# An attention-plus-MLP kernel rewritten: transposed Q, K and O, scores ahead of PV, paced side work

## The chip, the cores and the metric

The kernel runs on one core of a Trainium2 chip. The metric is the device time of one execution in microseconds (us). The profile tells apart a matrix engine (PE, or TensorE; the kernels here put its results into eight PSUM banks), ScalarE (ACT, which computes the exponentials here), VectorE (DVE), GpSimd (POOL) and queues for data movement. In the traces an engine takes its own instructions in the order of its queue and waits for the others: in the changed kernel ScalarE's normalisation of the third tile of x, whose inputs were ready at 10.6 us, started at 16.62 us, behind a copy of the tile before it that had waited 3.41 us for the PE. The profile also records the clock that the PE was granted; every record is either full or half (mean 0.617 before).

"Faster", "slower" and "same" below compare fast runs of two kernels on the same chip, in the same rounds. A ratio is the mean time of one kernel's fast runs over that of the other's of the same rounds, so it is not quite the ratio of the medians that stand beside it.

## The reference, cut to what matters

```python
xn = layernorm(x)                            # x: 2048 x 512, bf16
q = xn @ wq   # 32 heads of 16               k = xn @ wk ; v = xn @ wv   # one head of 16
p = softmax(q k^T / 4) ; o = p v             # 32 heads x 2048 x 2048 exponentials
out = x + o @ wo + (gelu(xn @ w1 + b1) @ w2 + b2)      # w1: 512 x 1792
```

The exponentials dominate: 32 x 2048 x 2048 of them, all on ScalarE in tiles of 128 rows, 948.7 us of the 1216.8 us span of the kernel before.

## The kernel before

A "chunk" is 512 query rows, one head with one query each: four heads by the same 128 queries. Three chunks form a group; a group takes 16 steps, one for each 128 keys. A step has three score matmuls (K is stationary, 17 rows: 16 for the head and one that subtracts a bound of the maximum), one exponential over three PSUM banks, and three PV matmuls that add up in the single O bank (V with a column of ones, so that row 16 of the result is the softmax denominator). There are 43 groups, 688 steps. The scores use six banks, two sets of three. All the rest of the PE's work (Q projection, GELU layer, output; "side work") uses the last bank.

```python
def plan_scores(s):          # three matmuls, side by side in three row strips of the array
    ...
        KT_sb[32*j:32*j+17, kt*P:(kt+1)*P], QT_sb[32*j:32*j+17, g % QT_RING, :]
def plan_PV(s):              # three matmuls side by side in three column strips, and a filler
    ...
        pO[32*j:32*j+17, :], V1[:, kt, :], E_sb[:, s % 2, j*512:(j+1)*512]
    if PV_FILL:
        pO[96:113, :], V1[:, kt, :], E_sb[:, s % 2, 0:512]       # its result is not used
def plan_O_evac(g):          # the O bank is free after these two
    t1 = tensor_copy(oc_hi, pO)                  # waits for the last PV of the group
    t_dveO[g] = tensor_tensor(oc_lo, pO, oc_hi, SUBTRACT)
...
for s in range(NS):          # order of the PE's queue
    plan_exp(s)
    plan_PV(s)
    if kt == KT - 1: plan_O_evac(g)
    if s + 2 < NS: plan_scores(s + 2)
    run_misc_slot(s)         # side work: now and then a burst, often of four or more matmuls
```

## Time and profile before

| | before |
|---|---|
| time | 1213.67 us, median of 3 (1209.01 to 1217.55) |
| first exponential starts, last ends | 65.0, 1207.4 us |
| ScalarE idle before exponentials, in between | 171 us |
| mean granted PE clock | 0.617 of full |

The page of the kernel before: its span, busy times (share of the span, number of instructions), the granted clock in tenths of full speed in 40 slices of the span, and some of the costliest groups. A group's line has the source line, engine, operation, result and inputs, sizes, count | busy us, mean ns | idle us of the engine just before, and who ended most of that.

```profile
span 1216.8 us, 14581 instructions
...
PE 960.1 (79%) x6411; PEld 237.8 (20%) x6477; DVE 356.8 (29%) x774; ACT 983.7 (81%) x763; POOL 99.1 (8%) x52
...
PEclk9855767668555557595666557755655595555555
...
L574 ACT ACTIVATE E_sb<-pAll 128x1536 bf16<-128x1536 f32 (+1 forms) x688 | 948.7, 1442 | 184.4 <-PE pAll L560 180.8
L593 PE MATMUL pAll<-E_sb,V 128*17 128x512 bf16 x2048 | 385.4, 552 | 118.5 <-ACT E_sb L574 115.8
L560 PE MATMUL pAll<-QT_sb,KT_sb 17*128 17x512 bf16 x2048 | 384.8, 553 | 0.0
...
L614 DVE CAST oc_hi<-pAll 128x512 bf16<-128x512 f32 x43 | 29.6, 689 | 258.2 <-PE pAll L598 258.2
...
L616 DVE TENSOR_TENSOR oc_lo<-pAll,oc_hi 128x512 bf16<-128x512 f32 x43 | 29.7, 691 | 1.5
```

ScalarE is the busiest engine and its exponentials waited 184 us in total, 181 of it for the scores (L560). The clock row shows 5 for most of the run: half clock, with stretches of full. The sum of idle time before the k-th exponential of a group, over all groups, is mine, from the trace: 72.7 us fall on the third exponential, 98 us on all others.

Timeline of the kernel before (start, length, engine, line, operation, count, idle before and who ended it); a burst of side-by-side matmuls is one line.

```profile
1165.12 0.60 PE L593 MATMUL pAll<-E_sb,V 128*17 128x512 bf16 x3 [0.21 <-ACT E_sb L574]
...
1165.78 0.69 DVE L614 CAST oc_hi<-pAll 128x512 bf16<-128x512 f32 x1 [18.75 <-PE pAll L598]
1166.50 0.69 DVE L616 TENSOR_TENSOR oc_lo<-pAll,oc_hi 128x512 bf16<-128x512 f32 x1
...
1167.71 0.60 PE L593 MATMUL pAll<-E_sb,V 128*17 128x512 bf16 x3
...
1168.25 0.61 PE L560 MATMUL pAll<-QT_sb,KT_sb 17*128 17x512 bf16 x3
...
1168.91 1.45 ACT L574 ACTIVATE E_sb<-pAll 128x1536 bf16<-128x1536 f32 x1 [1.14 <-PE pAll L560]
```

The last PV of the group (L593) starts at 1165.12. The two copies hold the O bank until 1167.2, the next PV starts at 1167.71, and the scores that ScalarE needs stand behind that PV: ScalarE is idle for 1.14 us.

### The profile page before, as it was taken

To read this page: it belongs to the slowest core of one execution; us is meant where nothing else is said; L and a number is where in the kernel's file an instruction comes from. 1 tells how busy PE (TensorE), PEld (TensorE's weight loads), DVE (VectorE), ACT (ScalarE), POOL (GpSimd) and SP (SyncE) were. 2 spreads that over 40 slices of the span, in tenths; PEclk is the share of its full clock that TensorE was granted. 3 is DMA by queue.
4 is the path that set the end of the run, shared out by engine and by line. 5 is a ranking of instruction groups with operands and counts; after the bars stand their busy time and mean duration, and the time that the engine had idled before them with its cause. 6 is when DMAs were issued, how large, how long until landed. Compare 5 with 4: busy or idle time off the path is not lost.

```text
span 1216.8 us, 14581 instructions
## 1 busy us (share of the span) xinstructions
PE 960.1 (79%) x6411; PEld 237.8 (20%) x6477; DVE 356.8 (29%) x774; ACT 983.7 (81%) x763; POOL 99.1 (8%) x52
## 2 busy tenths in 40 slices
PE   0578777779888887798887878888788888878887
PEld 0312122212112112121122112211122121111111
DVE  4634544431122344210244431112444121111101
ACT  0367879898987688899988789996887889988895
POOL 2268830000000000000000000000000000000000
PEclk9855767668555557595666557755655595555555
DMA  6000000000000000000000000000000000000000
GB/s 225 1 1 1 1 1 1 1 1 1 1 5 14 1 1 1 1 1 1 9 5 1 5 1 1 1 1 10 1 5 1 5 1 1 5 1 5 5 1 4
DMA packets 7326, 9.87 MB, mean 8 GB/s; under 512 B 448, under 2 KB 6880, under 8 KB 7264
## 3 DMA queue, kind: packets, MB, share of 16 engines
q1 hardware_dynamic: 6720, 6.55, 1.7%
q0 software_dynamic: 544, 2.40, 0.5%
q8 instruction: 50, 0.82, 0.3%
q14 instruction: 12, 0.10, 0.0%
HBM read 6.85 MB, written 2.10 MB: 7 GB/s over the span
## 4 chain that ended last, share of the span: by engine, by line
PE 43%; ACT 40%; DVE 11%; issue 3%; DMA 1%; POOL 1%; SPq 0%
ACT E_sb L574 39%; PE pAll L593 12%; PE pAll L560 11%; PE pAll L741 6%; PE pAll L794 5%; DVE oc_lo L616 2%; DVE oc_hi L614 2%; PE pAll L700 2%; PE pAll L508 2%; PE pAll L402 1%; DMA x_sb<-in_A_x_dram 1%; PE pAll L634 1%; POOL m_f L431 1%; ACT ub L767 1%; DVE xpy L802 1%
## 5 line engine op out<-in xcount | busy, mean ns | idle before, releaser
L574 ACT ACTIVATE E_sb<-pAll 128x1536 bf16<-128x1536 f32 (+1 forms) x688 | 948.7, 1442 | 184.4 <-PE pAll L560 180.8
L593 PE MATMUL pAll<-E_sb,V 128*17 128x512 bf16 x2048 | 385.4, 552 | 118.5 <-ACT E_sb L574 115.8
L560 PE MATMUL pAll<-QT_sb,KT_sb 17*128 17x512 bf16 x2048 | 384.8, 553 | 0.0
L598 PE MATMUL pAll<-E_sb,V 128*17 128x512 bf16 x688 | 379.2, 551 | 0.0
L593 PEld LDWEIGHTS pAll<-E_sb,V 128*17 128x17 bf16 x2048 | 69.4, 93 | 431.7 <-ACT E_sb L574 335.2
L560 PEld LDWEIGHTS pAll<-QT_sb,KT_sb 17*128 17x128 bf16 x2048 | 71.1, 97 | 272.1 <-issue 272.1
L614 DVE CAST oc_hi<-pAll 128x512 bf16<-128x512 f32 x43 | 29.6, 689 | 258.2 <-PE pAll L598 258.2
L748 DVE TENSOR_SCALAR hb<-pAll,b1T 128x512 bf16<-128x512 f32 x56 | 42.0, 751 | 184.0 <-PE pAll L741 184.0
L741 PE MATMUL pAll<-xnT,w_sb 128*128 128x512 bf16 x197 | 84.2, 567 | 10.1 <-issue 7.6
L431 POOL TENSOR_TENSOR m_f<-ssqR,half_sb 128x32 f32<-128x32 f32 x16 | 86.8, 5426 | 44.3 <-DVE ssqR L428 44.3
L794 PE MATMUL pAll<-w_sb,ub 128*128 128x512 bf16 x208 | 64.6, 415 | 6.6 <-DVE xpy L802 4.4
L598 PEld LDWEIGHTS pAll<-E_sb,V 128*17 128x17 bf16 x688 | 61.6, 90 | 0.0
L634 PE MATMUL pAll<-ident_b,oc_hi 81*128 81x51 bf16 (+1 forms) x172 | 19.6, 215 | 50.2 <-DVE oc_lo L616 48.3
L774 DVE SCALAR_TENSOR_TENSOR ub<-ub,hb 128x512 bf16<-128x512 bf16 x56 | 38.4, 686 | 44.8 <-ACT ub L767 44.8
L802 DVE TENSOR_TENSOR xpy<-pAll,x_sb 128x512 f32<-128x512 f32 x16 | 11.1, 692 | 110.2 <-PE pAll L798 110.2
L516 DVE CAST QT_sb<-pAll 81x512 bf16<-81x512 f32 (+1 forms) x43 | 29.5, 685 | 39.5 <-PE pAll L598 28.2
L508 PE MATMUL pAll<-ident_b,qx 128*17 128x128 bf16 x512 | 26.9, 298 | 17.0 <-POOL qx L434 9.6
L767 ACT ACTIVATE ub<-ub 128x512 bf16<-128x512 bf16 x56 | 35.2, 628 | 0.0
L285 ACT ACTIVATE xnT<-pAll 128x512 bf16<-128x512 f32 x16 | 9.6, 597 | 30.0 <-PE pAll L280 29.6
L707 DVE TENSOR_TENSOR outbuf<-pAll,xpy 128x512 bf16<-128x512 f32 x16 | 11.1, 692 | 75.4 <-PE pAll L700 75.4
L741 PEld LDWEIGHTS pAll<-xnT,w_sb 128*128 128x128 bf16 x224 | 22.4, 121 | 48.6 <-issue 42.6
L616 DVE TENSOR_TENSOR oc_lo<-pAll,oc_hi 128x512 bf16<-128x512 f32 x43 | 29.7, 691 | 1.5
(83 smaller groups left out, 372.6 us busy)
## 6 DMA issues: line engine op xcount, KB each, us to landing
x_sb<-in_A_x_dram SPq DMA_DIRECT2D x2, 1024.0 KB, 10.7
out_dram<-outbuf SPq DMA_DIRECT2D x16, 128.0 KB, 1.7
w_sb<-in_B_w_dram SPq DMA_DIRECT2D x1, 1792.0 KB, 19.8
w_sb<-in_B_w_dram POOLq DMA_DIRECT2D x1, 1792.0 KB, 12.4
wq_sb<-in_A_wq_dram POOLq DMA_DIRECT2D x1, 512.0 KB, 7.8
wo_sb<-in_A_wo_dram SPq DMA_DIRECT2D x1, 512.0 KB, 19.1
wkv_sb<-in_A_wk_dram POOLq DMA_DIRECT2D x1, 16.0 KB, 6.7
wkv_sb<-in_A_wv_dram POOLq DMA_DIRECT2D x1, 16.0 KB, 6.6
```

The lines of the kernel that those rows point to most:

```text
L431: tpw = add("pool", (lambda ti: lambda e: e.tensor_tensor(m_f[:, ti, :], ssqR[:, ti, :], half_sb[:, :], ALU.pow))(ti), waits=[("dve", tR), ...
L508: tk = add("pe", (lambda j, qb, tc, h: lambda e: e.matmul(pM[32 * j:32 * j + 17, qb * P:(qb + 1) * P], qx[:, tc, h, :], ident_b[:, :]))(j, ...
L560: tk = add("pe", (lambda j, X, kt, g: lambda e: e.matmul(pS[:, (3 * X + j) * 512:(3 * X + j + 1) * 512], KT_sb[32 * j:32 * j + 17, kt * P: ...
L574: t_actE[s] = add("act", (lambda X, n, s: lambda e: e.activation(E_sb[:, s % 2, 0:n * 512], pS[:, 3 * X * 512: 3 * X * 512 + n * 512], ACT ...
L593: tk = add("pe", (lambda j, kt, s: lambda e: e.matmul(pO[32 * j:32 * j + 17, :], V1[:, kt, :], E_sb[:, s % 2, j * 512:(j + 1) * 512], star ...
L598: tk = add("pe", (lambda kt, s: lambda e: e.matmul(pO[96:113, :], V1[:, kt, :], E_sb[:, s % 2, 0:512], start=(kt == 0), stop=(kt == KT - 1 ...
L614: t1 = add("dve", (lambda g: lambda e: e.tensor_copy(oc_hi[:, g % 2, :], pO[:, :]))(g), waits=waits, mark=True)
L616: t_dveO[g] = add("dve", (lambda g: lambda e: e.tensor_tensor(oc_lo[:, g % 2, :], pO[:, :], oc_hi[:, g % 2, :], ALU.subtract))(g), waits=[ ...
L741: tk = add("pe", (lambda d, ft, c0, c1, w, pb: lambda e: e.matmul(pb[:, 0:w], w1_sb[:, d, ft * P:(ft + 1) * P], xnT[:, d, c0:c1], start=(d ...
L748: th = add("dve", (lambda ft, w, pb: lambda e: e.tensor_scalar(hb[:, ft, 0:w], pb[:, 0:w], b1T[:, ft:ft + 1], None, ALU.add))(ft, w, pb), ...
L767: t_actT[(sc, ft)] = add("act", (lambda ft, w: lambda e: e.activation(ub[:, ft, 0:w], ub[:, ft, 0:w], ACT.Tanh, scale=GELU_K))(ft, w), wai ...
L794: tk = add("pe", (lambda ft, loc: lambda e: e.matmul(pM[:, :], ub[:, ft, loc * P:(loc + 1) * P], w2_sb[:, ft, :], start=(ft == 0), stop=Fa ...
```

## The change

Its intent: keep everything transposed so that no PE transposes are needed, put the scores ahead of PV in the PE's queue so that ScalarE's next exponential is never behind PV, pace the side work to two matmuls per step, and normalise in batches of four tiles. A new bookkeeper (`Prog`) derives the semaphore waits from what each operation reads (`r=`) and writes (`w=`). Groups are three heads by the same 512 tokens, so there are 4 x 11 groups (the eleventh has two heads) and 704 steps. The diff is 1449 lines; this is its core.

```diff
-            plan_exp(s)
-            plan_PV(s)
-            if kt == KT - 1: plan_O_evac(g)
-            if s + 2 < NS: plan_scores(s + 2)
-            run_misc_slot(s)
+            exp(s)
+            if s + 2 < NS:
+                scores(s + 2)
+            pv(s)                       # E has four buffers; no filler matmul
+            if kt == NT - 1:
+                o_evac(tb, g)
+            ...                         # tanh in threes, gates
+            while mi_live and n < PER_STEP and s >= gap_until:     # PER_STEP = 2
+                k = next(mi)            # one side matmul
...
+        def scores(s):
+                mm(bank(3 * x + j), KT[q0:q0 + 17, kt * P:(kt + 1) * P], QT[q0:q0 + 17, tb % 2, h // 4, :], ...)
+        def pv(s):
+                mm(pO[32 * j:32 * j + 32, :], V1[:, kt, :], E[:, s % NEB, j * TBW:(j + 1) * TBW], ...)
+        def o_evac(tb, g):
+            dve(stream_shuffle(den[0:n, i, :], pO[0:n, :], [16] * 32), w=[B(6), ("den", i)])
+            dve(reciprocal(den[0:n, i, :], den[0:n, i, :]), ...)
+            dve(tensor_tensor(oT[0:n, tb % 2, g, :], pO[0:n, :], den[0:n, i, :], MULT), w=[B(6), ...])
...
+        ln_batch(0); consts_dve(); ln_batch(1); k_block(0); ...; ln_batch(2); k_block(1); ln_batch(3); ...
```

B(6) is the O bank. All three operations of `o_evac` touch it or stand between two that do, so the next PV waits for all three. The padding rows 17 to 31 of KT and QT are zero, because the projection weights are padded with zero columns.

## The prediction

> **What bounds it now.** Page: span 1216.8 us, ScalarE (ACT) busy 984 (81%), PE 960 (79%). Groups: 672 exponentials of 128x1536, back to back every 1.35 us (timeline), 16 of 128x1024 at about 0.93, 56 tanh at about 0.53: a floor of about 952 us. The first exponential starts at 65 us, the last ends at 1207 (timeline, chain of waits). So ACT waits about 190 us in the loop, 181 of it on the scores. Two causes. (a) PE order PV, scores, then a side burst of four matmuls: when the clock is half (mean 0.617) PV takes 0.53, scores 0.54, a burst 1.8 us, and ACT loses 1.44 us, as at 83 to 112 us. (b) At each of 43 group ends the two O copies (0.69 + 0.69) hold the O bank, then eight transposes precede the next PV: about 1 us lost.
>
> **What the change does.**
> - Exponential work is unchanged: 640 of 1536, 64 of 1024, tanh in threes (20): about 950 us.
> - Prologue: the first exponential at about 45 us instead of 65. The GpSimd power (2 x 5.4 us) and K/Q transposes go; but the GpSimd half of the normalisation stands behind two large memsets (about 10 us, estimated from its small memsets), and ACT's in-order queue waits for it. -20.
> - Scores ahead of PV, at most two side matmuls per step: PE per step is 0.32 + 0.32 + 0.53 = 1.17 us at full clock, under 1.35: no loss. At half clock 0.53 + 0.54 + 0.96 = 2.0, over it. On average there are 1.07 side matmuls per step, so half-clock stretches remain PE bound. I give this 30 to 70 us, against 120 to 140 for (a) now.
> - Group end: shuffle 0.69, reciprocal, multiply 0.69 hold the O bank. The small reciprocals took 207 ns for 8 elements, 233 for 12, 253 for 16: about 155 + 6.4 ns per element, so 512 should take about 3.4 us. [...] The next PV can start about 5.6 us after the last exponential's end. ACT has three exponentials ready (4.1 us), then waits for PV, side work and scores: 2.4 to 3.7 us lost, and the 4 us of PE idleness also drop the clock. 43 x about 3 = 130 us against about 43 now.
> - Tail: about 44 Y/output matmuls are left after the last step: about 18 us against 9.
>
> Sum: 45 + 950 + 130 + 40 + 15 = 1180. I take 1178 us, 80% range 1105 to 1245. Chances: faster by over 2% 0.55, within 0.31, slower 0.14.
>
> **What would show it.** Right: the reciprocal group at 3 to 4 us each, 44 of them; ACT's idle time before exponentials in pieces of 2 to 4 us about every 25 us; PV waiting for the O multiply; first exponential at 40 to 50 us; between group ends, exponentials every 1.35 us in full-clock stretches. Wrong: a reciprocal near 0.7 us (then the group ends cost almost nothing, and about 1060 is right); ACT idle spread over all steps (then PE bounds it).
>
> **What would make it wrong.** A clock mostly at half: the Y stretches, two side matmuls in every step, then run at 2.0 us per step, and 1230 or more follows. VectorE work queued ahead of the O evacuation lengthens the hold.

## The result

The changed kernel took 1345.45 us (median of 4 runs, 1339.45 to 1357.83) against 1211.93 (4 runs): ratio 1.110, 95% interval 1.103 to 1.116. It is 11% slower. The result is correct.

The page of the changed kernel. L222 is a helper through which all of its matmuls go, so they are told apart by their tiles.

```profile
span 1340.7 us, 11668 instructions
...
PE 1061.3 (79%) x4964; PEld 208.6 (16%) x5029; DVE 447.0 (33%) x642; ACT 998.7 (74%) x758; POOL 17.4 (1%) x26
...
PEclk9655555555557865555556865555558655755557
...
L387 ACT ACTIVATE E<-pAll 128x1536 bf16<-128x1536 f32 (+1 forms) x704 | 953.8, 1425 | 285.9 <-PE pAll L222 277.1
L222 PE MATMUL pAll<-E,V 128*32 128x512 bf16 x2048 | 409.5, 575 | 178.5 <-DVE oT L401 178.5
L222 PE MATMUL pAll<-QT,KT 17*128 17x512 bf16 x2048 | 404.1, 567 | 39.3 <-ACT E L387 31.8
L400 DVE RECIPROCAL den<-den 96x512 f32<-96x512 f32 (+1 forms) x44 | 147.3, 3349 | 1.5
...
L399 DVE STREAM_SHUFFLE den<-pAll 96x512 f32<-96x512 f32 (+1 forms) x44 | 31.7, 720 | 0.0
L401 DVE TENSOR_TENSOR oT<-pAll,den 96x512 bf16<-96x512 f32 (+1 forms) x44 | 30.2, 686 | 1.5
```

Three things to read here. ScalarE's idle time before exponentials went up, from 184 to 286 us, nearly all of it waiting for the PE. The clock row is almost all fives. The reciprocal is one instruction of 3349 ns for each group, as predicted, and PV waited 178.5 us for the multiply (L401) that ends the hold of the O bank.

The timeline of the changed kernel around one group end, with the half-clock steps before it and the change to full clock after it:

```profile
709.14 0.61 PE L222 MATMUL pAll<-QT,KT 17*128 17x512 bf16 x3
...
709.68 0.61 PE L222 MATMUL pAll<-E,V 128*32 128x512 bf16 x3
709.80 1.45 ACT L387 ACTIVATE E<-pAll 128x1536 bf16<-128x1536 f32 x1 [0.60 <-PE pAll L222]
...
710.23 1.03 PE L222 MATMUL pAll<-wop,oT 96*128 96x512 bf16 x2
...
711.20 0.61 PE L222 MATMUL pAll<-QT,KT 17*128 17x512 bf16 x3
...
714.51 0.72 DVE L399 STREAM_SHUFFLE den<-pAll 96x512 f32<-96x512 f32 x1
715.26 3.35 DVE L400 RECIPROCAL den<-den 96x512 f32<-96x512 f32 x1
...
718.65 0.69 DVE L401 TENSOR_TENSOR oT<-pAll,den 96x512 bf16<-96x512 f32 x1
...
719.39 0.61 PE L222 MATMUL pAll<-E,V 128*32 128x512 bf16 x3 [3.48 <-DVE oT L401]
...
720.47 0.61 PE L222 MATMUL pAll<-QT,KT 17*128 17x512 bf16 x3
...
721.13 2.79 ACT L387 ACTIVATE E<-pAll 128x1536 bf16<-128x1536 f32 x2 [3.72 <-PE pAll L222]
...
727.72 0.39 PE L222 MATMUL pAll<-QT,KT 17*128 17x512 bf16 x3
...
728.16 16.23 ACT L387 ACTIVATE E<-pAll 128x1536 bf16<-128x1536 f32 x12 [0.38 <-PE pAll L222]
...
728.91 0.39 PE L222 MATMUL pAll<-QT,KT 17*128 17x512 bf16 x3
```

Between 709 and 714 a step takes 2.06 us (709.14 to 711.20): scores 0.54, PV 0.55, two side matmuls 0.97, and ScalarE is idle 0.60 us in each step. From 693 to 715 the PE is never free, and yet the clock stays at half: its records give half clock from 645.8 to 727.8. Then the same four bursts take 1.19 us (727.72 to 728.91) and ScalarE runs twelve exponentials without a stop. In between is the group end: shuffle at 714.51, reciprocal until 718.61, multiply until 719.34, next PV at 719.39, scores after it at 720.47, and ScalarE idle for 3.72 us.

All traces, read the same way. "At the group end" is the idle time before the fourth exponential of a group if scores go ahead of PV, before the third if PV goes first; "elsewhere" is that before all other exponentials. "No wait" is the time from the first exponential to the end of the last, less idle. All in us, one profiled execution each.

| kernel | span | clock | first exponential | idle at the group end | idle elsewhere | no wait | after the last |
|---|---|---|---|---|---|---|---|
| before | 1216.8 | 0.617 | 65.0 | 72.7 | 98 | 972 | 9.5 |
| changed | 1340.7 | 0.578 | 62.4 | 169.8 | 112 | 978 | 18.9 |

The difference of the spans, 124 us, is 97 at the group ends, 14 elsewhere, 6 of no wait, 9 after the last exponential, and -3 at the start.

### The profile page after: what moved, and what is told of

Read it like the earlier page. It is cut to its first block, busy times and chain, and to the rows that moved or that the text cites. A ratio compares the mean times of both kernels' runs of the same rounds, so it can differ in the third digit from the quotient of the medians.

```text
span 1340.7 us, 11668 instructions
## 1 busy us (share of the span) xinstructions
PE 1061.3 (79%) x4964; PEld 208.6 (16%) x5029; DVE 447.0 (33%) x642; ACT 998.7 (74%) x758; POOL 17.4 (1%) x26
## 4 chain that ended last, share of the span: by engine, by line
PE 61%; ACT 19%; DVE 17%; issue 2%; POOL 1%; DMA 0%; DVEq 0%
PE pAll L222 61%; ACT E L387 16%; DVE den L400 11%; DVE den L399 2%; DVE oT L401 2%; ACT ub L441 1%; PE pAll L298 0%; ACT xn L289 0%; ACT xnT L301 0%; POOL wop L257 0%; DVE stats L277 0%; DMA wk_s<-in_A_wk_dram 0%; POOL wqp L256 0%; ACT KT L311 0%; DVE outb L568 0%
## 5 line engine op out<-in xcount | busy, mean ns | idle before, releaser
L387 ACT ACTIVATE E<-pAll 128x1536 bf16<-128x1536 f32 (+1 forms) x704 | 953.8, 1425 | 285.9 <-PE pAll L222 277.1
L222 PE MATMUL pAll<-E,V 128*32 128x512 bf16 x2048 | 409.5, 575 | 178.5 <-DVE oT L401 178.5
L222 PE MATMUL pAll<-QT,KT 17*128 17x512 bf16 x2048 | 404.1, 567 | 39.3 <-ACT E L387 31.8
L400 DVE RECIPROCAL den<-den 96x512 f32<-96x512 f32 (+1 forms) x44 | 147.3, 3349 | 1.5
L222 PEld LDWEIGHTS pAll<-E,V 128*32 128x32 bf16 x2048 | 74.5, 100 | 466.0 <-issue 266.1
L222 PEld LDWEIGHTS pAll<-QT,KT 17*128 17x128 bf16 x2048 | 72.8, 97 | 464.4 <-ACT E L387 260.8
L222 PE MATMUL pAll<-xnT,w_sb 128*128 128x512 bf16 x196 | 102.3, 610 | 8.6 <-issue 8.6
L222 PE MATMUL pAll<-w_sb,ub 128*128 128x512 bf16 x209 | 91.3, 534 | 5.4 <-issue 4.6
L222 PE MATMUL pAll<-wop,oT 96*128 96x512 bf16 (+1 forms) x176 | 66.8, 468 | 0.0
L222 PE MATMUL pAll<-xnT,wqp 128*128 128x512 bf16 x108 | 57.5, 621 | 3.7 <-issue 3.7
L399 DVE STREAM_SHUFFLE den<-pAll 96x512 f32<-96x512 f32 (+1 forms) x44 | 31.7, 720 | 0.0
L401 DVE TENSOR_TENSOR oT<-pAll,den 96x512 bf16<-96x512 f32 (+1 forms) x44 | 30.2, 686 | 1.5
L441 ACT ACTIVATE ub<-ub 128x1536 bf16<-128x1536 bf16 (+1 forms) x20 | 27.9, 1393 | 0.1
```

Source lines behind the costliest of these rows:

```text
L222: return add("pe", lambda e: e.matmul(o, l, rh, start=start, stop=stop, **kw), r, w)
L387: act(lambda e: e.activation(E[:, s % NEB, 0:n * TBW], bank(3 * x, n), ACT.Exp, scale=0.25), w=[B(3 * x + i) for i in range(3)] + [("E", s ...
L399: dve(lambda e: e.stream_shuffle(den[0:n, i, :], pO[0:n, :], [16] * 32), w=[B(6), ("den", i)])
L400: dve(lambda e: e.reciprocal(den[0:n, i, :], den[0:n, i, :]), r=[("den", i)], w=[("den", i)])
L401: dve(lambda e: e.tensor_tensor(oT[0:n, tb % 2, g, :], pO[0:n, :], den[0:n, i, :], ALU.mult), r=[("den", i)], w=[B(6), ("oT", tb % 2, g)])
L441: act(lambda e: e.activation(ub[:, f0:f0 + n, :], ub[:, f0:f0 + n, :], ACT.Tanh, scale=GELU_K), r=[("u", f) for f in fts], w=[("u", f) for ...
```

## The experiments

Two theories stood at first. H: the O bank is held too long, and the rest follows from it. C: the half clock binds the PE, and the hold hardly matters. For the clock itself, A: the granted clock follows the share of the array's cells at work (rows times columns); B: it follows the PE's busy time; and later R: it follows the share of the array's rows at work. The medians of the kernel before differ a little (1212 to 1219 us), so compare the ratios; a difference in us below, unless it says otherwise, is one of medians and may be off by some us.

### e1_copyout: hold the bank for one copy only

```diff
-            dve(stream_shuffle(den, pO, [16] * 32), w=[B(6), ("den", i)])
+            dve(tensor_copy(oc, pO), w=[B(6), ("oc", i)])
+            dve(stream_shuffle(den, oc, [16] * 32), r=[("oc", i)], w=[("den", i)])
             dve(reciprocal(den, den), ...)
-            dve(tensor_tensor(oT, pO, den, MULT), w=[B(6), ("oT", tb % 2, g)])
+            dve(tensor_tensor(oT, oc, den, MULT), w=[("oT", tb % 2, g)])
```

(The waits that keep `oc` from being overwritten too early are left out here.)

> The O bank is first copied to SBUF (0.69 us) and the shuffle, the reciprocal (3.35 us) and the multiply read the copy, so the bank is held about 0.7 us instead of 4.8. Theory H (the hold is what costs): ScalarE's idle time at the fourth exponential of a group, 170 us now, falls under 40, and the time falls by about 130 us to 1190 to 1220, near the kernel before. Theory C (the half clock is what costs): the PE idleness goes too, but the PE then has to do its work at half clock; 704 steps of 1.07 us plus about 780 side matmuls of 0.48 are 1130 us, plus 62 of prologue and 19 of tail, so it does not get under about 1210 unless the clock rises, and idle time moves to the other exponentials.

Measured: 1195.57 us (1188.11 to 1214.42; the longest run was slow, and the ratio leaves it out), ratio to the kernel before 0.979 (0.972 to 0.986): faster, but whether by more than 2% is unclear. Clock 0.615. Idle at the group end 8.7 us instead of 170, elsewhere 117 instead of 112. The timeline of this version at a group end:

```profile
633.58 0.69 DVE L400 COPY oc<-pAll 96x512 f32<-96x512 f32 x1 [15.93 <-PE pAll L223]
...
634.36 0.40 PE L223 MATMUL pAll<-E,V 128*32 128x512 bf16 x3
...
635.06 3.35 DVE L402 RECIPROCAL den<-den 96x512 f32<-96x512 f32 x1
```

The next PV starts at 634.36, right after the copy; the reciprocal runs beside it. Theory H gave the number (1190 to 1220). Theory C's floor of 1210 us was passed. C allowed for that if the clock rose, and it did a little (0.578 to 0.615), but C also had the idle time move to the other exponentials, and it did not. So the hold accounts for 150 us of the changed kernel (1345 less 1196), more than the whole loss. The idle time elsewhere is about the same in sum (117 us), though not in its parts: see the end of the experiments.

### e2_rows32 and e3_filler: the same work on more of the array

```diff
# e2_rows32, in scores(s)
-    mm(bank(3 * x + j), KT[q0:q0 + 17, ...], QT[q0:q0 + 17, ...], ...)
+    mm(bank(3 * x + j), KT[q0:q0 + 32, ...], QT[q0:q0 + 32, ...], ...)   # rows 17 to 31 are zero
# e3_filler, at the end of pv(s)
+    mm(pO[96:128, :], V1[:, kt, :], E[:, s % NEB, 0:TBW], ...)           # a fourth column strip
```

Both add work on rows and columns of the array that the changed kernel does not use, and by the traces at no time: at half clock a step without a wait and with two side matmuls takes 2.05 us (median) in the changed kernel and in e2_rows32, and what follows a PV burst starts 0.54 us after it with the fourth strip (1167.71 to 1168.25 in the kernel before) and 0.55 without it (709.68 to 710.23 in the changed one). Two side matmuls one after the other take 0.97 us.

> The score matmuls take 32 rows instead of 17; rows 17 to 31 of K and Q are zero, so the result is the same and a matmul streams for the same 512 columns. Theory A (the granted clock follows the share of array cells that work in a window of 3.4 us): at half clock the saturated step with one side matmul on average goes from 0.59 to 0.69 of the cells and the one with two from 0.66 to 0.73, over the 0.65 to 0.7 at which windows of both traces went to full clock; mean clock from 0.58 to over 0.68 and the time down by 40 to 100 us. Theory B (the clock follows PE busy time only, or work on zeros does not count): clock 0.56 to 0.60 and time within 1%.

> A fourth PV matmul per step into the unused 32 columns (as the kernel before has); it runs beside the other three and its result is not read. Theory A: cells at half clock go from 0.59 to 0.66 (one side matmul) and 0.66 to 0.71 (two), so the clock rises, somewhat less than with 32 score rows: mean 0.62 to 0.72, time down by 20 to 70 us. Theory B: no change within 1%.

Measured: e2_rows32 1257.66 us (1253.91 to 1264.48), ratio 1.033 (1.028 to 1.038), clock 0.734; idle at the group end 162 us, elsewhere 47. e3_filler 1337.87 us (1333.88 to 1340.82), ratio 1.098 (1.093 to 1.102), clock 0.577; idle 172 and 106. From the pages of e2_rows32 and then e3_filler, the granted clock in 40 slices:

```profile
PEclk9867767776568876766757887776867787776579
```

```profile
PEclk9555555555577576555557675555555675556568
```

Fifteen more rows of zeros in each score matmul took 88 us off (1345 to 1258). Of the 87 us between the spans, 65 come from the idle time away from the group ends, 13 from exponentials that follow one another more often, and 8 from the group ends, where the hold (162 us) stands nearly as before. A fourth column strip did nothing to the clock: three of its four runs have 0.577 to 0.584, and the fourth, recorded at 0.659, was no faster (1340.82 us). So B falls: the streaming time of a step was the same. A falls too: e3_filler was to gain 20 to 70 us and gained about 8 (1338 against 1345; 15 by the ratios). R is what is left of the three: 15 more rows in each score matmul raised the clock of the changed kernel from 0.578 to 0.734, a fourth column strip left it at 0.577 to 0.584 in three runs of four. Going from 17 to 32 rows in each strip is the only step of rows that was tried.

This can be seen in the windows of the trace. In the traces of both kernels all granted-clock records but the last are multiples of 3.41 us long. I cut each trace into these windows and added up, for those at half clock, the share of rows at work: a score burst counts 3 x 17 or 3 x 32 rows of 128 (the most that a matmul has in these pages) for as long as it streams, a PV burst all 128 (with three strips or four), a side matmul all its rows. The table gives how many windows were followed by one at full clock, of how many. It is an estimate: about 1% of the matmul records were missing and were put in from the weight loads.

| rows at work in a half-clock window | under 0.65 | 0.65 to 0.73 | 0.73 to 0.76 | 0.76 and over |
|---|---|---|---|---|
| changed | 0 of 241 | 0 of 69 | 4 of 10 | 11 of 11 |
| e3_filler | 0 of 244 | 1 of 64 | 10 of 16 | 6 of 6 |
| e2_rows32 | 0 of 104 | 2 of 30 | 11 of 23 | 38 of 38 |
| before | 0 of 184 | 2 of 31 | 0 of 18 | 18 of 40 |

By this count the border is at about 0.74 in the changed kernel and its variants. A saturated step there, at half clock, has 0.40 (scores) + 1 (PV) + n (side matmuls) times 0.427 us of streaming (512 columns at half clock: in the kernel before, the later matmuls of a side burst of four start 0.427 us apart there, 0.216 at full clock). With one side matmul in 1.51 us (median of 25 such steps) that is 0.68 of the rows, with two in 2.05 us 0.71. Both lie under the border, and the PE that was never free from 693 to 715 us stayed at half clock. With 32 score rows both are 0.78, over it. (Without a side matmul, in 1.09 us, it is 0.55 and 0.69, under it in both.) The same count by busy time shows no border: in the changed kernel 172 half-clock windows had the PE streaming for at least 80% of the time, and only 15 were followed by full clock.

In the kernel before, 22 windows over 0.76 stayed at half in this count. A second count of the same traces took each burst, with its filler, as 0.427 us; there the kernel before has 0 of 234 windows under 0.73, 0 of 15 up to 0.76 and 20 of 25 over it, so most of the 22 come from the way of counting. Over all thirteen traces it gives 4 of 2565 under 0.73, 76 of 207 up to 0.76 and 303 of 354 over it. In full-clock windows the changed kernel fell back in 15 of 15 under 0.35 and in none of 28 over 0.40. The same count also settles whether theory A could be saved by another border: of the windows with 0.63 to 0.71 of the cells at work, 16 of 41 were followed by full clock in the kernel before and none of 72 in e3_filler. Still, 51 windows over 0.76 stayed at half, so what exactly the granted clock follows stays open.

### e4_pvfirst: the old order in the new kernel

```diff
+            pv(s)
             if s + 2 < NS:
                 scores(s + 2)
-            pv(s)
```

> The PE order of the kernel before (PV, then scores, then side matmuls) in the changed kernel. If the new order (scores first) brings what it was meant for, this is slower by 30 to 60 us: at full clock scores come 0.32 us later and at the group ends the score matmul stands behind a PV that waits for the O bank one step earlier, so about 1.3 us more per group end. If the PE is the bound at half clock between group ends, the order matters there little, and only the group ends lengthen.

Measured: 1407.98 us (1400.89 to 1423.53, the longest left out of the ratio), ratio 1.160 (1.151 to 1.168), so 63 us slower than the changed kernel, clock 0.569. Idle at the group end, now before the third exponential, 175.5 us, elsewhere 155. The new order was worth what it was meant for; the surprise is that it gained away from the group ends (155 against 112), not at them.

### e5_co_r32: both repairs

Both edits of e1_copyout and e2_rows32.

> Both at once: O copied out first, and 32 score rows. If the hold and the clock are the two causes, and separate, the idle time at the fourth exponential stays near 9 us and that at the others near 45 us, so 62 us of prologue, about 955 of exponential and tanh time, 60 of idle and 18 of tail: 1085 to 1110 us. If the hold was what kept the clock low (or the reverse) the gains overlap and it stays over 1130. The clock should be about 0.73 or more.

Measured: 1109.22 us (1106.68 to 1111.03), ratio to the kernel before 0.911 (0.905 to 0.917), clock 0.784. Idle at the group end 1.2 us, elsewhere 61. From its page:

```profile
span 1107.8 us, 11715 instructions
...
PEclk9967786686658997866678999688767899785589
...
L388 ACT ACTIVATE E<-pAll 128x1536 bf16<-128x1536 f32 (+1 forms) x704 | 936.3, 1499 | 66.3 <-PE pAll L223 59.9
```

ScalarE's exponentials now wait 66 us where they waited 286. The single gains were 150 and 88 us, their sum 238; the two together gained 236 (by the ratios 159 and 94, their sum 253, and 242 together). So they are two nearly separate causes of the changed kernel's time. Only the hold is new in it: the kernel before has 17 score rows too, as b3_rows32 shows below.

### b1_nofill, b2_hold and b3_rows32: the same causes in the kernel before

```diff
# b1_nofill
-        PV_FILL = True
+        PV_FILL = False
# b2_hold, in plan_O_evac (dummy: 512 f32 ones per lane, set once in the prologue)
     t1 = tensor_copy(oc_hi, pO)
+    t1 = reciprocal(dummy, dummy)            # after the copy; the subtract waits for it
     t_dveO[g] = tensor_tensor(oc_lo, pO, oc_hi, SUBTRACT)
# b3_rows32 (kx padded from 17 to 32 columns with zeros, K and Q copied with 32 rows)
-    KT_sb[32*j:32*j+17, ...], QT_sb[32*j:32*j+17, ...]
+    KT_sb[32*j:32*j+32, ...], QT_sb[32*j:32*j+32, ...]
```

> The kernel before without its fourth PV matmul. The fourth one adds columns, not rows. If the clock follows the share of array rows that work (theory R, which the last runs left standing: 32 score rows raised the clock, the filler columns did not), clock 0.60 to 0.63 and the time within 1.5%. If columns count, the clock falls to 0.55 to 0.58 and the time rises by 3% or more.

> The kernel before with a reciprocal of 512 elements (on a scratch tile) between its two O copies: the O bank is held 4.8 us instead of 1.4. Theory H: 3.35 us more at each of 43 group ends, less what slack there is (none: scores there stand behind PV), so 110 to 150 us more: 1320 to 1365 us, about the time of the changed kernel, and the idle time at the third exponential of a group goes from 73 to 190 to 220 us. Rival (the hold is hidden in the kernel before): under 50 us more.

> The kernel before with 32 score rows instead of 17 (rows 17 to 31 of K are zero, those of Q hold finite leftovers; same result). Theory R: at half clock a step with PV and scores alone goes from 0.44 to 0.55 of the rows, with a burst of four side matmuls in a window from about 0.74 to 0.80, so windows with a burst go to full clock; mean clock from 0.62 to 0.68 or more and the time falls by 20 to 80 us. If the effect is something particular to the changed kernel, no change.

Measured: b1_nofill 1215.63 us, ratio 0.999 (0.992 to 1.005), clock 0.636 (its runs 0.611 to 0.636, those of the kernel before beside it 0.611 to 0.639): the filler of the kernel before did nothing. b2_hold 1369.38 us (1365.71 to 1385.27), ratio 1.127 (1.118 to 1.136); idle before the third exponential 218 us instead of 73, and 115 elsewhere. That is 153 us for 43 reciprocals of 3.35 us, 3.6 each, slightly more than expected: a hold of the changed kernel's length makes the kernel before as slow as the changed one. Two groups of b2_hold, the exponentials and the added reciprocals:

```profile
L576 ACT ACTIVATE E_sb<-pAll 128x1536 bf16<-128x1536 f32 (+1 forms) x688 | 949.2, 1441 | 346.8 <-PE pAll L562 343.5
...
L618 DVE RECIPROCAL dctr<-dctr 128x512 f32<-128x512 f32 x43 | 144.2, 3353 | 1.5
```

b3_rows32 1173.68 us (1172.06 to 1177.42), ratio 0.964 (0.959 to 0.970), clock 0.701; idle elsewhere 61 us instead of 98, at the group end 69. So the rows work in the kernel before as well, and it was itself 3.6% slower than it had to be.

### e9_pvfirst: what the order is worth once both are repaired

The edit of e4_pvfirst on e5_co_r32.

> The version with both repairs (O copied out, 32 score rows), but with PV ahead of the scores as in the kernel before. With the bank held 0.7 us only and the clock higher, this shows what the order itself is worth: at a group end PV waits for the copy about 0.8 us, and with scores behind it ScalarE waits too; at half clock two side matmuls plus PV stand ahead of the scores. Expected 25 to 70 us slower than 1109; if the order is worth nothing here, within 10.

Measured: 1144.58 us (1139.98 to 1148.53), ratio 0.939 (0.932 to 0.945), clock 0.752: 35 us slower than e5_co_r32. The order of the changed kernel is right, and worth about 3%.

### e7_prolog and e8_tail: start and end

In the changed kernel VectorE's queue up to the start of the third batch of the normalisation, and GpSimd's memsets, read in the timeline of VectorE and then of GpSimd:

```profile
6.85 3.07 DVE L281 TENSOR_SCALAR ve_b<-mv 128x4 bf16<-128x4 f32 x1
...
10.87 3.89 DVE L269 COPY sel<-mask 128x32 bf16<-128x32 bf16 x1
...
26.59 0.41 DVE L313 TENSOR_TENSOR sqk<-KT 16x512 bf16<-16x512 bf16 x1 [6.89 <-ACT KT L311]
27.71 0.69 DVE L316 TENSOR_REDUCE kmax<-pAll 128x1 f32<-128x512 f32 x1 [0.70 <-PE pAll L222]
...
28.51 2.47 DVE L277 BATCH_NORM_STATS2 stats<-x_sb 128x6 f32<-128x512 bf16 x4
```

```profile
6.37 3.53 POOL L256 MEMSET wqp<- 128x4096 bf16 x1
9.84 4.82 POOL L257 MEMSET wop<- 96x5632 bf16 x1
14.66 1.52 POOL L293 TENSOR_SCALAR xn<-x_sb,rstd,nmr 128x512 bf16<-128x512 bf16 x2
```

The statistics of the third batch (28.51) stand behind the K maximum of the first block (27.71), which waits for PE and ScalarE. Nothing there waits for x. The prediction had put the delay down to the memsets. They held GpSimd's half of the first normalisation up from about 10.6 to 14.66 us, and VectorE was slow beside them as well: the copy of 32 elements above took 3.89 us, ending within 0.1 us of GpSimd's 4.82 us memset, and took 0.68 us in e7_prolog, where GpSimd has no large memset; in the same way an operation on 4 elements of the first statistics took 3.07 us beside the memset before it, and 0.17 us in e7_prolog. Why is not shown. Together with GpSimd's 4.1 us, the 2.9 us of that operation are about 7 us of delay in the first batch (an estimate from these two traces). e7_prolog moves the statistics and the normalisation of all batches ahead of the K maxima and gives the two memsets to VectorE, before x arrives. e8_tail adds one edit to it:

```diff
-        LASTG = NGR - 2
+        LASTG = NGR - 4        # the last four output tiles start earlier
```

> Both repairs, and the prologue reordered: VectorE's statistics of all four batches go ahead of the K maxima in its queue, and the two large memsets go from GpSimd to VectorE's idle start. The trace of the changed kernel shows each batch of statistics standing behind the K maximum of an earlier block, about 12 us per batch. Expected: first exponential at 38 to 46 us instead of 62, time 1085 to 1095. If the memsets alone were the cause, as the prediction had it, the first exponential comes about 4 us earlier only.

> As e7_prolog, and the last four output tiles start four groups before the end instead of two, so that nearly no Y matmuls are left for after the last exponential: tail 10 to 12 us instead of 17 to 19, time 5 to 10 us less than e7_prolog, about 1078 to 1090.

Measured: e7_prolog 1093.49 us (1091.89 to 1094.71), ratio 0.898 (0.893 to 0.903); first exponential at 45.7 us. e8_tail 1085.68 us (1083.67 to 1086.79), ratio 0.891 (0.887 to 0.896); 15.6 us after the last exponential, where 10 to 12 were expected. The 8 us came all the same, but not where they were expected: between the two profiles the tail gave 1.6 us and the idle time elsewhere 5.5. e8_tail is the fastest version: 10.9% faster than the kernel before, correct, and with the changed kernel's structure. From its page:

```profile
span 1085.1 us, 11714 instructions
...
PEclk9878857766568998665868899687766899866997
...
L403 ACT ACTIVATE E<-pAll 128x1536 bf16<-128x1536 f32 (+1 forms) x704 | 936.3, 1493 | 61.7 <-PE pAll L223 55.4
```

Of its remaining idle time, 24.5 us fall on the sixth exponential of a group. That is a price of copying out: the sixth had 7.4 us in the changed kernel, 27.9 in e1_copyout and 25.6 in e5_co_r32. Now the PE runs on while VectorE is at the reciprocal (3.35 us), and its side matmuls come to wait for VectorE work behind it: the list of waits of e5_co_r32 has the PE's weight loads waiting 16.9 us for the square of Q. That this is the cause was not tried.

All variants in one table, as that above:

| kernel | ratio to before | span | clock | first exponential | idle at the group end | idle elsewhere | after the last |
|---|---|---|---|---|---|---|---|
| changed | 1.110 | 1340.7 | 0.578 | 62.4 | 169.8 | 112 | 18.9 |
| e1_copyout | 0.979 | 1186.4 | 0.615 | 62.7 | 8.7 | 117 | 17.3 |
| e2_rows32 | 1.033 | 1253.9 | 0.734 | 62.6 | 162.0 | 47 | 17.1 |
| e3_filler | 1.098 | 1336.1 | 0.577 | 63.2 | 172.1 | 106 | 17.2 |
| e4_pvfirst | 1.160 | 1399.2 | 0.569 | 62.6 | 175.5 | 155 | 17.4 |
| e5_co_r32 | 0.911 | 1107.8 | 0.784 | 62.6 | 1.2 | 61 | 17.3 |
| e9_pvfirst | 0.939 | 1146.8 | 0.752 | 62.2 | 4.0 | 91 | 17.3 |
| e7_prolog | 0.898 | 1091.0 | 0.783 | 45.7 | 1.2 | 61 | 17.3 |
| e8_tail | 0.891 | 1085.1 | 0.783 | 45.7 | 2.2 | 55 | 15.6 |
| b1_nofill | 0.999 | 1208.2 | 0.636 | 64.7 | 73.2 | 91 | 9.5 |
| b2_hold | 1.127 | 1383.3 | 0.604 | 65.1 | 218.4 | 115 | 12.9 |
| b3_rows32 | 0.964 | 1172.3 | 0.701 | 64.6 | 68.9 | 61 | 9.5 |

## Why the prediction was wrong

The prediction leaned to faster (1178 us, chance of slower 0.14). The measured time, 1345 us, lies outside its range. Its sum, term by term, against the profiled execution:

| term | predicted | measured |
|---|---|---|
| up to the first exponential | 45 | 62.4 |
| exponentials and tanh, no waits | 950 | 978 |
| group ends | 130 | 170 |
| PE bound at half clock, elsewhere | 40 | 112 |
| after the last exponential | 15 | 18.9 |
| sum | 1180 | 1341 |

- **The step that failed most** is "I give this 30 to 70 us" for the half-clock stretches; 40 stood in the sum, 112 was measured. The cost per step was right (2.0 us predicted, 2.06 in the timeline). What was wrong was how many steps would be at half clock. The prediction gives no number; with its average of 1.07 side matmuls a half-clock step takes about 0.53 + 0.54 + 0.51 = 1.58 us, 0.23 over the 1.35 of an exponential, so its 40 us mean some 170 steps (an estimate). 597 of 704 exponentials started at half clock, and the trace of the kernel before already had 536 of 688. The prediction named a clock mostly at half as what would make it wrong, "and 1230 or more follows", but gave it too little weight. Its one reason for a lower clock, the PE's 4 us of idleness at a group end, is in the trace (six group ends of the changed kernel came at full clock, the PE was idle there for 4.0 us, and it went on at half clock after each), but it was not what held the clock down: e1_copyout took that idleness away and the clock rose from 0.578 to 0.615 only. The runs gave another: rows at work, 0.68 to 0.71 in a saturated half-clock step with side matmuls against a border of about 0.74 (e2_rows32, b3_rows32, and e3_filler against columns).
- **The group ends**: the mechanism was right in each part. The reciprocal was put at 3.4 us, worked out from the three small reciprocals at about 6.4 ns per element, and took 3.35: 3349 ns, where a multiply of the same size took 686. The term was mis-sized: "43 x about 3" was 3.9 each. The likely reason is that all 43 came at half clock, where PV, side work and scores after the hold take longer; in the kernel before the 37 at half clock lost 1.9 us each, the 6 at full clock 0.6. And "about 43 now" was 73 for the kernel before (1.7 each). So the net loss at the group ends, 97 us, was nearly what was predicted (87). It is this term that made the kernel slower: it was called in the prediction, and outweighed by a gain elsewhere that did not come.
- **The gain that did not come**: "30 to 70 us, against 120 to 140 for (a) now". The kernel before lost 98 us away from the group ends, not 120 to 140, and the changed one 112. The paced side work replaced bursts that stalled ScalarE, but the bursts, it seems, had also pushed windows over the border (no run changed the pacing alone, so this is not shown): in the kernel before 20 of 273 half-clock windows were followed by full clock, in the changed one 15 of 331.
- **Exponentials without waits**: 950 against 978. An exponential that follows a wait takes 1.45 us, one that follows another starts 1.35 us after it (both timelines). That is 0.1 us less. 216 waits, as the profile's list has them, times 0.1 us are 22 of the 28 us. A term for waits should carry this 0.1 us each.
- **The start**: "-20" came out as -3. The GpSimd memsets were only part of the cause: VectorE's queue order was the other (e7_prolog moved both and brought the first exponential 16.9 us earlier; the estimate above puts about 7 us of the delay on the memsets, and no run parts the two).
- **Right**: one reciprocal of 3.35 us for each of 44 groups, PV waiting for the O multiply, idle pieces at each group end (3.2 to 4.6 us, where 2 to 4 were named), back-to-back exponentials in full-clock stretches (728 to 744), and the long tail (18.9 against 18 in its text, though 15 stood in its sum).

## What to carry to other kernels

Price a PSUM bank's hold from the last matmul that writes it to the last instruction that reads it, and copy the bank out before anything slow, above all a reciprocal over hundreds of elements per lane: here one of 512 took 3.35 us, and one 0.69 us copy was worth 150 us. When a trace shows the PE saturated and still at half clock, as from 693 to 715 us here, do not assume that saturation will bring the full clock; try more array rows, since padding the contraction from 17 to 32 rows per strip with zeros left the step at 2.05 us and gave 3.6% in one kernel and about 6.5% in the other. Put the matmuls that the busiest engine waits for first in the PE's queue (3 to 5% here), and check each engine's queue order in a prologue for work that could have gone ahead.
